# First expert of a mixture layer by block products, last feed-forward group reordered by token block, token sums spread over the expert's units

## The chip, the cores and the metric

One core of a Trainium2 chip (trn2). The metric is the device time of one execution in microseconds (us). An execution of the kernel before takes 1540.04 us, the median of three (1538.99 to 1540.66).

## The reference, cut to what matters

The kernel computes three layers in a row on 1536 tokens of width 512. The attention ahead of them is not touched by the change.

```python
def _moe_ref(x, w_in, w_out):            # 512 -> 2048 -> 512
    h = x @ w_in
    sp = np.where(h > 20.0, h, np.log1p(np.exp(np.minimum(h, 20.0))))
    return (h * np.tanh(sp)) @ w_out     # "Mish"

def _moe2_ref(x, w_gate, w1, w2):        # N=1536, D=512, E=8 experts, F=1024
    logits = x @ w_gate
    logits = logits - logits.max()
    P = np.exp(logits)
    for _ in range(8):
        P /= P.sum(1, keepdims=True) + 1e-09
        P /= P.sum(0, keepdims=True) + 1e-09
        P *= N / E
    out = np.zeros((N, D))
    for e in range(E):
        out += P[:, e:e + 1] * (np.maximum(x @ w1[e], 0.0) @ w2[e])
    return out
```

The loop of eight rounds divides the 1536 x 8 table P by its row sums and then by its column sums. It is called the normalisation below.

## The kernel before, in words

Numbers are fp32, split into a high and a low fp32r part; a product of two numbers is three matmuls (high x high, high x low, low x high). The program is written out by hand, with one in-order queue for each engine: PE (matmuls), DVE, ACT, POOL, and SP for DMAs.

**Attention** ends at about 267 us and leaves the tokens in `xh` and `xl` (4 chunks of 128 features x 1536 tokens).

**Steps.** The feed-forward layer (16 chunks of 128 hidden features) and the first of the eight experts (8 chunks) run as steps. A step is one chunk i and one block tb of 512 tokens: `up(n)` issues 12 matmuls of 128x512, `act(n)` forms the hidden values (ACT) and their low part `gl` (DVE), and three steps later (LAG) `down(n)` issues 12 matmuls into four PSUM banks y0 to y3. Four chunks make a group, and the steps run over groups, then token blocks, then chunks: 48 steps of the layer and 24 of the first expert. After the last chunk of a group `evacuate` adds the four banks to `acc` (DVE). After the last group of the layer, `split` writes the new `xh` (ACT) and `xl` (POOL).

The layer's weights are 64-bit numbers that are decoded on the way (`decode`: 2 ACT, 5 DVE and 1 POOL operation for half a chunk), and put as two parts into one of eight ring buffers (`convert_hi` on ACT, `convert_lo` on POOL). The table `early` says in which step that is done.

`at(n, f)` appends work to the end of step n. In the steps of the first expert stand: the eight matmuls of `logits` for each token block, the eight rounds of the normalisation on 32 partitions (`sinkhorn`, one round in each step), `spread` (four DMAs that bring P to 128 partitions), and `make_t`, which forms the sums and differences of tokens ("T" factors) that the next part needs.

**Units.** The other seven experts run by block products: of each group g of 768 tokens and each quarter k of an expert's hidden features, `product` computes seven products (six matmuls of 128x384 each) in place of eight, into two PSUM banks; after each, `post` reads its bank (ACT: `p1`, `c11`; DVE: `u`, `v`, `c22`, `c21`, `c12`). A bank is used by every second product, so product 3 waits until `u` was read after product 1, product 5 until `v` was read after product 3, and so on. DVE then forms four low parts (`rest`, tile `gl`), and `second` issues 36 matmuls of 128x512 into six banks. An expert's four units end with six `gather` (P times bank, added to `acc`). There are 56 units: seven experts for 768 tokens, then the same for the other 768. The weights of a unit are prepared one or two units ahead (`unit_a`, `unit_s`, `unit_w`: copies on ACT, sums and low parts on POOL). `job(u, s, f)` appends work behind product s of unit u (s from 0 to 6), or behind quarter s - 7 of its `second`.

Units and steps use the same PSUM banks and, for the even units, ring buffers 0 to 2.

Of the kernel before, what the change touches and what calls it, by code (L numbers as in the profile page):

```python
# [61 lines left out]
def lsh_attention_moe_kernel(  # L62
# [780 lines left out]
    def act(n):  # L843
        g = step(n)[0]
# [3 lines left out]
        if g < NG:  # L848
            a = t_p.tile([P, TB], F32, tag="t", name="t")
            nc.scalar.activation(a, t, AF.Mish)  # L850
            nc.scalar.copy(hi, a)  # L851
            nc.vector.tensor_sub(lo, a, f32(hi))  # L852
        else:
            nc.scalar.activation(hi, t, AF.Relu)
            nc.vector.scalar_tensor_tensor(
                out=lo, in0=t, scalar=0.0, in1=f32(hi), op0=ALU.max, op1=ALU.subtract
            )
        hid[n] = (hi, lo)

    def down(n):  # L860
# [3 lines left out]
        for j in range(KC):  # L864
# [4 lines left out]
            if g < NG:  # L869
                ops = [(w0[:, c], hi), (w0[:, c], lo), (w1[:, c], hi)]  # L870
            else:
                ops = [(hi[:, c], w0), (hi[:, c], w1), (lo[:, c], w0)]
            for m, (x, y) in enumerate(ops):
# [487 lines left out]
```

## Time and profile before

| what | us |
|---|---|
| median of three executions | 1540.04 |
| the profiled execution: its time | 1540.54 |
| the profiled execution: span of its instructions | 1538.7 |
| PE busy in the span | 1524.6 (99%) |
| DVE, ACT, POOL busy | 879.9, 677.8, 880.3 |
| chain that ended last, by engine | PE 92%, DVE 3%, DMA 2% |

Busy times are sums over the span. The chain is followed back from the last instruction: at each step to what released it. In rows of the trace the columns are the start in us from the span's first instruction, the duration in us, the engine and line, the operation, out<-in, the shape, and in brackets how long the engine was idle ahead of it and who ended that.

### The profile page before, as it was taken

Reading aid. Unit: us, or ns where it says so; the run is one execution under the profiler, and the core shown is the slowest. Engines: PE = TensorE matmul, PEld = TensorE weight load, DVE = VectorE, ACT = ScalarE, POOL = GpSimd, SP = SyncE. Lnnn points to the kernel's source line nnn. Section 1 sums busy time; section 2 is a strip of 40 time slices with the busy share of each in tenths; the row PEclk is TensorE's granted clock in tenths of the full one; section 3 lists DMA queues with packets and bytes.
Section 4 is the critical chain, followed back from the end, with each engine's and each line's share of the span. In section 5 each row is a group of like instructions: output and inputs, shape, how many; then the busy total and the mean of one; then the engine's idle time right before and its main releaser. Section 6 shows DMA issues by size and latency. Waiting matters only on the chain.

```text
span 1538.7 us, 20305 instructions
## 1 busy us (share of the span) xinstructions
PE 1524.6 (99%) x7444; PEld 1341.9 (87%) x7444; DVE 879.9 (57%) x1434; ACT 677.8 (44%) x1230; POOL 880.3 (57%) x729
## 2 busy tenths in 40 slices
PE   9999999999999999999999999999999999999999
PEld 7798888888888788889999998989898989898998
DVE  8899995846663238666444454676534444445353
ACT  5777777654433232233434333333433333333331
POOL 6798977333324230266666666666666666666661
PEclk9999999999999999999999999999999999999999
DMA  7755550122221000112222222222322222221211
GB/s 184 160 138 148 140 133 16 55 71 67 69 69 55 28 28 1 29 56 69 69 69 69 69 69 69 69 69 69 110 69 69 68 66 67 65 67 68 69 56 41
DMA packets 64387, 113.50 MB, mean 74 GB/s; under 512 B 19792, under 2 KB 20792, under 8 KB 64288
## 3 DMA queue, kind: packets, MB, share of 16 engines
q1 hardware_dynamic: 62688, 112.17, 25.2%
q8 instruction: 58, 0.95, 0.3%
q14 instruction: 41, 0.34, 0.1%
q10 hardware_dynamic: 1600, 0.05, 0.0%
HBM read 89.22 MB, written 3.15 MB: 60 GB/s over the span
## 4 chain that ended last, share of the span: by engine, by line
PE 92%; DVE 3%; DMA 2%; POOL 1%; issue 1%; ACT 1%; SPq 0%; DVEq 0%; ACTq 0%; POOLq 0%
PE y L1224 30%; PE u L1157 27%; PE y L874 13%; PE pav L496 5%; PE h L840 4%; PE h L838 4%; PE h L839 4%; PE pst L446 1%; PE pst L447 1%; PE ps L394 1%; DMA vt<-in_v_dram 1%; DVE mx L408 1%; DMA raw<-in_qk_dram 1%; POOL plo L458 0%; PE lg L900 0%
## 5 line engine op out<-in xcount | busy, mean ns | idle before, releaser
L1165 ACT ACTIVATE gh<-c 128x384 fp32r<-128x384 f32 x224 | 117.8, 526 | 153.1 <-DVE c L1177 151.3
L1177 DVE TENSOR_TENSOR u<-u,p 128x384 f32<-128x384 f32 x56 | 31.2, 558 | 264.3 <-PE u L1157 264.3
L1170 DVE SCALAR_TENSOR_TENSOR gl<-c,gh 128x384 fp32r<-128x384 f32 x224 | 170.0, 820 | 0.0
L1224 PE MATMUL y<-ww,gh 128*128 128x512 f32 x672 | 163.4, 391 | 0.0
L1224 PE MATMUL y<-w,gh 128*128 128x512 f32 x672 | 162.6, 391 | 0.0
L458 POOL TENSOR_TENSOR plo<-p,ph 128x384 fp32r<-128x384 f32 x128 | 138.8, 1096 | 33.0 <-ACT ph L455 19.1
L1224 PEld LDWEIGHTS y<-w,gh 128*128 128x128 f32 x672 | 125.8, 188 | 25.1
L1224 PEld LDWEIGHTS y<-ww,gh 128*128 128x128 f32 x672 | 125.8, 188 | 25.1
L153 POOL TENSOR_TENSOR stage<-stage,sgn 128x512 f32<-128x512 f32 x32 | 43.1, 1346 | 120.8 <-DVE sgn L151 113.4
L1046 POOL TENSOR_TENSOR w<-stage,w 128x1024 fp32r<-128x1024 f32 x28 | 67.0, 2392 | 78.4 <-ACT w L1042 78.4
L874 PE MATMUL y<-gh,w 128*128 128x512 f32 x336 | 110.3, 389 | 0.0
L452 ACT ACTIVATE p<-pst 128x384 f32<-128x384 f32 x192 | 92.6, 487 | 38.3 <-PE pst L447 32.3
L1046 POOL TENSOR_TENSOR ww<-stage,ww 128x1024 fp32r<-128x1024 f32 x28 | 67.2, 2402 | 72.6 <-ACT ww L1042 72.6
L1039 POOL TENSOR_TENSOR w<-sraw,w 128x1024 fp32r<-128x1024 f32 x28 | 68.6, 2448 | 67.7 <-ACT w L1035 67.7
L408 DVE TENSOR_REDUCE mx<-ps 128x1 f32<-128x768 f32 x95 | 90.1, 948 | 15.5 <-PE ps L394 14.8
L838 PE MATMUL h<-xh,w 128*128 128x512 f32 x252 | 98.4, 391 | 0.0
L840 PE MATMUL h<-xh,w 128*128 128x512 f32 x252 | 98.2, 390 | 0.1
L839 PE MATMUL h<-xl,w 128*128 128x512 f32 x252 | 98.1, 389 | 0.0
L1022 POOL TENSOR_TENSOR wa<-stage,wa 128x512 fp32r<-128x512 f32 x28 | 40.2, 1436 | 96.8 <-ACT wa L1017 69.1
L852 DVE TENSOR_TENSOR gl<-t,gh 128x512 fp32r<-128x512 f32 x48 | 47.7, 994 | 77.5 <-ACT gh L851 77.5
L1042 ACT CAST ww<-stage 128x1024 fp32r<-128x1024 f32 x28 | 29.4, 1051 | 141.0 <-PE y L1224 141.0
L1042 ACT CAST w<-stage 128x1024 fp32r<-128x1024 f32 x28 | 29.4, 1050 | 138.2 <-PE y L1224 138.2
(243 smaller groups left out, 4069.1 us busy)
## 6 DMA issues: line engine op xcount, KB each, us to landing
stage<-in_w_dram SPq DMA_DIRECT2D x152, 512.0 KB
raw<-in_qk_dram SPq DMA_DIRECT2D x13, 384.0 KB
wx<-hi SPq DMA_DIRECT2D x20, 192.0 KB
vt<-in_v_dram SPq DMA_DIRECT2D x16, 192.0 KB
out_dram<-acc SPq DMA_DIRECT2D x11, 256.0 KB
zq<-hi SPq DMA_DIRECT2D x11, 192.0 KB
ak<-hi SPq DMA_DIRECT2D x11, 192.0 KB
zq<-lo SPq DMA_DIRECT2D x11, 192.0 KB
```

The source lines that it names most:

```text
L408: nc.vector.tensor_reduce(out=m[:, t, 0:1], in_=s_t[t][:, :, :HALF], axis=AX.XY, op=ALU.max, negate=True)
L452: nc.scalar.activation(p_t[u, c], st_t.pop((u, c))[:, :HALF], AF.Exp, scale=0.125)
L458: (nc.gpsimd if e == "P" else nc.vector).tensor_sub(out, in0, in1)
L838: nc.tensor.matmul(t, wt[:, 0, f], xh[:, kc, c], start=(kc == 0), stop=False)
L839: nc.tensor.matmul(t, wt[:, 0, f], xl[:, kc, c], start=False, stop=False)
L840: nc.tensor.matmul(t, wt[:, 1, f], xh[:, kc, c], start=False, stop=(kc == KC - 1))
L874: nc.tensor.matmul(yps[j], x, y, start=(head and m == 0), stop=(tail and m == 2))
L1046: nc.gpsimd.tensor_sub(y[:, 1, :], t, f32(y)[:, 0, :])
L1157: nc.tensor.matmul(bank[x], weight(u, a, m, kc), moving(u, b, mm, kc), start=(first and n == 0), stop=(n == 5), skip_group_check=not first)
L1165: nc.scalar.activation(hi, src, AF.Relu)
L1170: nc.vector.scalar_tensor_tensor(out=lo, in0=src, scalar=0.0, in1=f32(hid_u[u, c][0]), op0=ALU.max, op1=ALU.subtract)
L1224: nc.tensor.matmul(y_t[t], (hi, hi, lo)[m][:, t % 3 * P:(t % 3 + 1) * P], y, start=(k == 0 and first), stop=(k == NF // 2 - 1 and last),)
```

## The change

The first expert leaves the steps and joins the units: 48 steps remain, and 64 units (first expert first). The last two groups of the layer run over token blocks 0 and 1 first, and then both over block 2. The T factors of the first 768 tokens, which come from blocks 0 and 1, are made during steps 43 to 48. The logits of block 2, and the normalisation, now on 128 partitions and split into a half for rows (4 DVE operations) and a half for columns (13 DVE operations, eight of them transpositions of 32x32), stand in units 0 to 6. P is final in unit 6, so for the first 768 tokens the first expert's banks are stored as they are and scaled by six `scale_first` in unit 7; for the others `gather` multiplies at once. `spread` is gone. The decode table steps by 1.35 steps for half a chunk instead of 1.5.

```diff
-    NW = N64 + NF
-    NU = 2 * (E - 1) * NF // 2
+    NU = 2 * E * NF // 2
...
-    GROUPS = [list(range(i, i + FG)) for i in range(0, NW, FG)]
-    steps = [(g, tb, i) for g, c in enumerate(GROUPS) for tb in range(NTB) for i in c]
+    GROUPS = [list(range(i, i + FG)) for i in range(0, N64, FG)]
+    turns = [(g, tb) for g in range(NG - 2) for tb in range(NTB)]
+    turns += [(g, tb) for g in (NG - 2, NG - 1) for tb in range(2)] + [(g, 2) for g in (NG - 2, NG - 1)]
+    steps = [(g, tb, i) for g, tb in turns for i in GROUPS[g]]
...
     def across(x, op, negate=False):
-        y, r = small("y", Q), small("r")
-        nc.vector.transpose(out=y, in_=x)
+        y, r = small("y", Q, P), small("r", Q)
+        for a, part in enumerate(quarters(x)):
+            nc.vector.transpose(out=y[:, a * Q:(a + 1) * Q], in_=part)
         nc.vector.tensor_reduce(out=r, in_=y, axis=AX.X, op=op, negate=negate)
         return r
...
     def sinkhorn_max():
+        m = small("m", P)
+        nc.vector.tensor_reduce(out=m, in_=prob, axis=AX.XY, op=ALU.max)
+        r = across(m.to_broadcast([P, Q]), ALU.max, negate=True)
+        m = small("nm", P)
+        for part in quarters(m):
+            nc.vector.tensor_copy(part, r)
+        return m
...
-    for it in range(8):
-        at(n0 + 3 + it, sinkhorn)
-    at(n0 + 12, spread)
+    done_at = {tb: n + LAG for n, (g, tb, _) in enumerate(steps) if g == NG - 1}
+    for tb in range(NTB - 1):
+        at(done_at[tb] + 3, logits, tb)
...
-    for x in range(8):
-        at(t0 + 4 + x, make_t, (1, 2, 4, 3)[x % 4], x // 4)
+    for n, k, kc in ((1, 1, 0), (2, 2, 0), (2, 4, 0), (3, 3, 0), (4, 1, 1), (4, 2, 1), (5, 4, 1), (6, 3, 1)):
+        at(done_at[1] + n, make_t, k, kc)
+    at(free[RING] - 2, unit_s, 0)
+    for f, i in ((unit_w_hi, 0), (unit_w_lo, 0), (unit_s_hi, 1), (unit_s_lo, 1), (unit_a_hi, 2), (unit_a_lo, 2)):
+        at(free[RING + i] + 1, f, 0)
+    at(free[RING + 2] + 2, unit_s, 1)
...
-                nd += 1.5
+                nd += 1.35
...
+        if e == 0:
+            nc.vector.tensor_scalar(out=dst, in0=y_t[t], scalar1=prob[:, i, 0:1] if g else 1.0, scalar2=None, op0=ALU.mult)
+            return
...
-    for i in range(NT):
-        job(i // 3, NP1 + 1 + i % 3, scale_first, i)
+    job(0, NP1 + 1, logits, NTB - 1, ps_u, "u0")
+    job(0, NP1 + 2, put("m", sinkhorn_max))
+    job(1, 0, lambda: sinkhorn_exp(box["m"]))
+    for x in range(16):
+        job(1 + x // 3, (2, NP1 + 1, NP1 + 1)[x % 3], (sinkhorn_rows, sinkhorn_cols)[x % 2])
+    for i in range(NT // 2):
+        job(7, NP1 + i // 3, scale_first, i)
```

So the row and column halves alternate: units 1 to 5 hold three halves each, one behind product 2 and two behind the second quarter of `second`, and unit 6 the last one. Behind product 2 stands a row half in units 1, 3 and 5, and a column half in units 2, 4 and 6.

**First place: DVE, the end of the steps.** Of the changed program, from the T factors of steps 47 and 48 (`t`, `tw`) over the last evacuation (`acc`) to the first operation of unit 0 (`u`). Lines are those of the changed file.

```order
L983 TENSOR_TENSOR t<-xh,xl 128x384
L984 TENSOR_TENSOR t<-t 128x384
L989 TENSOR_TENSOR tw<-t,tw 128x384
L978 TENSOR_TENSOR t<-xh 128x384
L979 TENSOR_TENSOR t<-xl 128x384
L980 TENSOR_TENSOR t<-t 128x384
L989 TENSOR_TENSOR tw<-t,tw 128x384
L866 TENSOR_TENSOR acc<-y_5699,acc 128x512
L866 TENSOR_TENSOR acc<-y_5703,acc 128x512
L866 TENSOR_TENSOR acc<-y_5707,acc 128x512
L866 TENSOR_TENSOR acc<-y_5711,acc 128x512
L1152 TENSOR_TENSOR u<-u,p_5813 128x384
```

The order of the kinds is that of before, where the T factors were spread over eight steps, of which the last was the last step with an `up`; now they are packed into six steps, of which the last has only a `down`.

**Second place: ACT, the same stretch.** From the last two steps with an `up` (L841 is Mish, L842 the high part `gh`) over the copies of T factors (L988) and of unit 0's weights (L996, L997) and the new `xh` of block 2 (L871) to `p1`, the copy after product 0 (L1159).

```order
L841 ACTIVATE t<-h 128x512
L842 CAST gh<-t 128x512
L988 CAST tw<-t 128x384 x2
L996 CAST wx_78<-stage 128x512
L997 CAST wx_78<-stage 128x256
L841 ACTIVATE t<-h 128x512
L842 CAST gh<-t 128x512
L988 CAST tw<-t 128x384 x2
L871 CAST xh<-acc 128x512 x4
L1159 COPY p_5813<-u 128x384
```

Before, the same place reads so:

```order
L854 ACTIVATE gh<-h 128x512
L1009 CAST tw<-t 128x384
L1184 COPY p_6728<-u 128x384
```

Four copies that each read one addition of the last evacuation now stand ahead of `p1`.

**Third place: DVE in units 0 to 2.** First from the end of unit 0 (the logits `lg`, their maximum, `nm` as the offset of the exponential) to `u` of unit 1, and then from `u` to `v` of unit 2.

```order
L887 STREAM_TRANSPOSE lgs<-lg 32x128 x4
L888 TENSOR_TENSOR prob<-lgs 128x32
L905 TENSOR_REDUCE m<-prob 128x1
L899 STREAM_TRANSPOSE y<-m 32x32 x4
L900 TENSOR_REDUCE r<-y 32x1
L909 COPY nm<-r 32x1 x4
L1152 TENSOR_TENSOR u<-u,p_5987 128x384
```

```order
L1152 TENSOR_TENSOR u<-u,p_6141 128x384
L923 TENSOR_REDUCE csum<-prob 128x8
L899 STREAM_TRANSPOSE y<-csum 32x32 x4
L900 TENSOR_REDUCE r<-y 32x1
L925 TENSOR_SCALAR r<-r 32x1
L926 RECIPROCAL r<-r 32x1
L929 STREAM_TRANSPOSE i<-r 32x32 x4
L930 SCALAR_TENSOR_TENSOR prob<-i,prob 128x96
L1152 TENSOR_TENSOR v<-u,p_6141 128x384
```

Before, `v` followed `u` at once in every unit (but for one `gather` where an expert had just ended).

## Rows read from the trace of the kernel before

**Rows 1.** The page, part 1: busy us, share of the span, instructions.

```profile
PE 1524.6 (99%) x7444; PEld 1341.9 (87%) x7444; DVE 879.9 (57%) x1434; ACT 677.8 (44%) x1230; POOL 880.3 (57%) x729
```

**Rows 2.** Waits of PE: us in total, times, longest; first of ten rows.

```profile
PE prow L427 <- DVE col L415: 2.5, 4, 1.3
```

**Rows 3.** Busy time by stretch: the steps, then the units.

```profile
267.10:665.10 398.00, 397.91 (x1754) 327.09 (x1753) 223.33 (x374) 152.03 (x242) 114.74 (x70) 1.00 0.15 46
665.10:1538.70 873.60, 869.75 (x4370) 788.27 (x4368) 429.09 (x631) 330.14 (x564) 552.39 (x436) 1.00 0.22 69
```

**Rows 4.** Timeline, PE: product 0 and product 5 of the first unit, product 0 of the last.

```profile
665.17 0.33 PE L1157 MATMUL u<-xh,wx 128*128 128x384 f32 x1
...
670.40 1.20 PE L1157 MATMUL u<-tw,wx 128*128 128x384 f32 x6
...
1519.18 0.33 PE L1157 MATMUL u<-xh,wa 128*128 128x384 f32 x1
```

**Rows 5.** Timeline, DVE and ACT: last evacuation, then `p1`, `u`, `v` of the first unit.

```profile
663.33 2.73 DVE L884 TENSOR_TENSOR acc<-y,acc 128x512 f32<-128x512 f32 x4 [4.79 <-PE y L874]
...
666.43 0.48 ACT L1184 COPY p<-u 128x384 f32<-128x384 f32 x1 [8.49 <-PE u L1157]
...
667.54 0.56 DVE L1177 TENSOR_TENSOR u<-u,p 128x384 f32<-128x384 f32 x1 [1.48 <-PE u L1157]
...
669.56 0.56 DVE L1177 TENSOR_TENSOR v<-u,p 128x384 f32<-128x384 f32 x1 [1.46 <-PE u L1157]
```

**Rows 6.** Groups by line and form, ACT, 500 to 700 us: busy us, mean ns | idle.

```profile
L890 ACT CAST xh<-acc 128x512 fp32r<-128x512 f32 x8 | 5.0, 622 | 1.3 <-DVE acc L887 1.0
L1009 ACT CAST tw<-t 128x384 fp32r<-128x384 f32 x8 | 4.1, 513 | 24.9 <-DVE t L1005 13.0 <-DVE t L1001 11.9
L850 ACT ACTIVATE t<-h 128x512 f32<-128x512 f32 x4 | 2.4, 598 | 15.8 <-PE h L840 15.8
L1017 ACT CAST wa<-stage 128x512 fp32r<-128x512 f32 x2 | 1.2, 614 | 0.0
```

**Rows 7.** Timeline, DVE and POOL: a `make_t` that meets `unit_s`.

```profile
634.76 1.76 DVE L999 TENSOR_TENSOR t<-xh 128x384 f32<-128x384 f32 x1
...
639.12 1.13 DVE L1010 TENSOR_TENSOR tw<-t,tw 128x384 fp32r<-128x384 f32 x1 [0.58 <-ACT tw L1009]
...
637.18 0.94 POOL L1030 TENSOR_TENSOR sraw<-sraw,stage 128x256 f32<-128x256 f32 x1
```

**Rows 8.** One line each, DVE: duration ns min/median/max, first and last start.

```profile
L950 DVE TENSOR_SCALAR acc<-acc,prob x12: 474/960/2612, 677.2 to 727.6; 128x512 f32<-128x512 f32 x12
L455 DVE CAST ph<-p x29: 311/492/1273, 34.7 to 264.9; 128x384 fp32r<-128x384 f32 x29
L522 DVE STREAM_TRANSPOSE rs<-nr x16: 557/566/579, 59.6 to 270.4; 128x384 f32<-128x384 f32 x16
```

**Rows 9.** POOL: busy in a stretch; one row; groups by line, 500 to 720 us.

```profile
670.60:695.20 24.60, 24.36 (x17) 1.00 0.33 104
...
681.77 2.59 POOL L1039 TENSOR_TENSOR w<-sraw,w 128x1024 fp32r<-128x1024 f32 x1
...
L891 POOL TENSOR_TENSOR xl<-acc,xh 128x512 fp32r<-128x512 f32 x8 | 10.6, 1353 | 23.5 <-ACT xh L890 23.5
```

**Rows 10.** Groups by line and form, DVE, 500 to 700 us: the normalisation.

```profile
L934 DVE TENSOR_REDUCE csum<-pr 32x8 f32<-32x384 f32 x8 | 7.0, 875 | 0.3
L930 DVE TENSOR_REDUCE rsum<-pr 32x48 f32<-32x384 f32 x8 | 4.2, 530 | 0.0
L940 DVE SCALAR_TENSOR_TENSOR pr<-i,pr 32x384 f32<-32x384 f32 x8 | 4.4, 547 | 0.3
L915 DVE STREAM_TRANSPOSE y<-csum 32x32 f32<-32x32 f32 x8 | 1.6, 200 | 0.3
L916 DVE TENSOR_REDUCE r<-y 32x1 f32<-32x32 f32 x9 | 1.6, 174 | 0.3
L937 DVE RECIPROCAL r<-r 32x1 f32<-32x1 f32 x8 | 1.2, 151 | 0.3
```

More of the change, by code (lines that the diff above doesn't have):

```diff
@@ L162, in source @@
     def source(i):
-        return dec[i % NDEC] if i < N64 else staged[i]
+        return dec[i % NDEC]
     def convert_hi():
@@ L847, in act @@
         lo = g_p.tile([P, TB], F32R, tag="gl", name="gl")
[L848 to L857, printed above, removed]
+        a = t_p.tile([P, TB], F32, tag="t", name="t")
+        nc.scalar.activation(a, t, AF.Mish)
+        nc.scalar.copy(hi, a)
+        nc.vector.tensor_sub(lo, a, f32(hi))
         hid[n] = (hi, lo)
@@ L868, in down @@
             w0, w1 = wt[:, 0, 512:1024], wt[:, 1, 512:1024]
[L869 to L873, printed above, removed]
+            for m, (x, y) in enumerate(((w0[:, c], hi), (w0[:, c], lo), (w1[:, c], hi))):
                 nc.tensor.matmul(yps[j], x, y, start=(head and m == 0), stop=(tail and m == 2))
@@ L937, in sinkhorn @@
         nc.vector.reciprocal(out=c, in_=c)
[L938 to L939 removed]
+        i = small("i", P, Q)
+        for part in quarters(i):
+            nc.vector.transpose(out=part, in_=c.to_broadcast([Q, Q]))
         nc.vector.scalar_tensor_tensor(
[L941 removed]
+            out=prob, in0=i[:, 0:E].unsqueeze(1).to_broadcast([P, NT, E]), scalar=float(NTOK // E), in1=prob, op0=ALU.mult, op1=ALU.mult
         )
[L944 to L946 removed]
     def scale_first(i):
@@ L965, in lsh_attention_moe_kernel @@
     LAG = 3
-    blk = NTB * NF
-    start_e = NG * NTB * FG
-    for tb in range(NTB):
-        n0 = start_e - (NTB - 1 - tb) * FG + LAG + 2
-        at(n0, logits, tb)
-    at(n0 + 1, put("m", sinkhorn_max))
-    at(n0 + 2, lambda: sinkhorn_exp(box["m"]))
-    for it in range(8):
-        at(n0 + 3 + it, sinkhorn)
-    at(n0 + 12, spread)
+    done_at = {tb: n + LAG for n, (g, tb, _) in enumerate(steps) if g == NG - 1}
+    for tb in range(NTB - 1):
+        at(done_at[tb] + 3, logits, tb)
     tw = []
@@ L1081, in lsh_attention_moe_kernel @@
     convert_lo()
-    for i in range(RING_A + NX + 1, NW):
+    for i in range(RING_A + NX + 1, N64):
         need = free[i - RING] + 1 if i >= RING else 0
-        if NATT <= i < N64:
+        if NATT <= i:
             nd = max(nd, free_dec.get(i - NDEC, 0))
@@ L1105, in lsh_attention_moe_kernel @@
                 decode(*t)
-        first = n >= LAG and step(n - LAG)[0] < NG and step(n - LAG)[4]
+        first = n >= LAG and step(n - LAG)[4]
         if first:
@@ L1120, in lsh_attention_moe_kernel @@
             f()
-    assert not side, side.keys()
+    assert not side and not early and not later, (side.keys(), early.keys())
     blocks.close()
@@ L1132, in lsh_attention_moe_kernel @@
     ))
+    sk_p.append(pool("sk", bufs=1))
+    wide_t = lambda: sk_p[0].tile([P, TB], F32, tag="wide", name="lgs")
     def weight(u, name, m, kc):
```

81 lines of the change are left out of this document (27 added, 54 removed).

## The prediction

> **What bounds the kernel now.** I read the busy times first: PE works 99% of the span [rows 1]. Then PE's waits: the largest of ten entries is 2.5 us, all of them in the attention [rows 2]. Then the two stretches that the change touches: in the steps PE is busy 397.9 of 398.0 us, and in the units nothing but the end is idle [rows 3]. So PE is the bound, it never waits there, and any wait that the change makes adds to the time in full. Work on the other engines is free only while it keeps inside the gaps that PE leaves it, so the question is how wide these gaps are.
>
> In a unit they are narrow. Product 5 starts 5.23 us after product 0 [rows 4], so a product takes 1.05 us, and product 3 starts at 3.14. `u` ends at 2.93 and `v` at 4.95, counted from the unit's start [rows 5]. Product 5 overwrites what `v` reads, so `v` has 0.28 us to spare. Work that is put between `u` and `v` on DVE is free up to 5.23 - 0.1 for the hand-over - 0.56 - 2.93 = 1.64 us. Beyond that, each us costs one.
>
> **What is gained.** The steps issue 72 x 24 matmuls, and 24 of the logits, in 398.0 us [rows 3]: 0.2272 us each. The first expert's 24 steps are 576 matmuls, 130.9 us. Eight units replace them at (1519.18 - 665.17) / 55 = 15.53 us each [rows 4], 124.2 us. The gain is 6.6 us. The logits cost the same wherever they stand.
>
> **The end of the steps.** Call T the end of the last `down`. Before, the last evacuation starts 1.84 us ahead of it and ends 0.89 behind it [rows 5]; `p1` runs at once when product 0 is done. Product 2 needs `p1`, at T + 2.1.
> Now the queue ahead is fuller (first and second place). Step 46 evacuates too; it ends 8.2 + 5.45 = 13.6 us ahead of T (three steps with only `down`, one full step), and by the same pattern DVE is free from T - 12.7. From there it has two `gl` at 0.69 (as an addition of the same size [rows 5]) and 14 operations of T factors at 0.56 (as `u` [rows 5]): 9.2 us. To it come waits:
> - four times 0.58 us for the ACT copy in a `make_t` [rows 7]: 2.3;
> - step 47's `gl`: on ACT its Mish and copy stand behind the last T copy and the two copies of `unit_a` (0.61, some 0.4, 0.60, 0.62 [rows 6]); DVE has only 0.56 us to do meanwhile, so it waits 1.7;
> - POOL: where a `make_t` met `unit_s`, its four operations took from 634.76 to 640.25, 5.5 us instead of 2.8 [rows 7]. The four operations of `unit_s` of unit 1 meet the last seven here. In those rows the tail of a longer POOL operation is in the first 1.76 us; without it I take 1.7, between 0 and 2.7.
>
> So the last evacuation starts at -12.7 + 9.2 + 2.3 + 1.7 + 1.7 = T + 2.2 and ends at T + 4.9. Now the copy of `xh` (0.62 [rows 6]) and `p1` (0.48 [rows 5]) follow: T + 6.0 instead of T + 2.1. **PE waits 3.9 us**; 2.2 without POOL, 4.9 with all of it.
>
> **From unit 0 to unit 1.** With that wait and 1.8 us of logits, unit 0 lasts 21.2 us, and unit 1's product 3 wants `u` read at T + 24.4. The logits end at T + 3.9 + 7.3 + 4.1 + 1.8 = T + 17.1. Four transpositions (about 0.3 each, between 32 and 384 columns [rows 8, 10]), the maximum, four more and a reduction bring DVE, with 0.03 between operations, to T + 20.0; the addition and the four copies to `nm` alone would end by T + 20.6. That is in time.
> But POOL does not pause there. Before, it was busy 24.4 of 24.6 us from 670.6 on, T + 5.4 to T + 30 [rows 9], and the change puts four more subtractions of 1.35 us in front [rows 9]. DVE operations that copy or scale from SBUF to SBUF, or read two SBUF tiles, wait for a running POOL operation: scaling takes 0.47 us alone and 2.61 beside a POOL operation of 2.59 us [rows 8, 9], and a cast from 0.31 to 1.27 [rows 8]. Transpositions don't: 16 of them, in a stretch where POOL is mostly busy, took 557 to 579 ns [rows 8]. The addition and the four copies are five operations of the waiting kinds, and each meets one POOL operation, of 24.36 / 17 = 1.43 us on average [rows 9]: 7.2 us, `u` ends at T + 28.4, and **PE waits 4.1 us**. No row shows a copy of one element beside POOL; if such a copy is too small to wait, the cost is 0. I take 4.1, since the nearest row, the cast, waits.
> [...]
>
> **Column halves between `u` and `v`** (third place; units 2, 4, 6). The price of a column half: the reduction of 96 elements 0.32 (0.875 for 384 [rows 10], with the 0.15 of the smallest operation as the fixed part), eight transpositions at 0.20 + 0.03, a reduction 0.17, two of 0.15, the product of 96 elements 0.25 (0.547 for 384, same fixed part), and gaps: 3.0 us. Two of the 13 are of the waiting kinds; `unit_s` runs there in pieces of about 0.74, so I add 0.2. The room is 1.64: **1.55 us in each of three units, 4.65 us**. In unit 4 a `gather`, about 0.7 us, stands ahead of it: **0.7 more**. Ends: 0.5 us each, if transpositions overlap, and 3.2 each, if both of them wait for a whole piece of 0.9.
>
> **The rest.** A row half (four operations, 0.95 us) fits into 1.64; with its two waits for POOL it is slightly late: 0.1 in units 1, 3 and 5, 0.3 in all; at most 0.8 each. Two halves behind the second quarter of `second` are 4.0 us and start some 11 us into the unit, with 6.9 us until the next `u`: 0, and if POOL's longest operation (2.6 us) is met, still 0. Six `scale_first` in unit 7: 6 x 0.47 and waits of 3.6 us are 6.4, in the same room: 0. The 12 new stores by `gather` stand where other experts' stand: 0. The decode's faster pace has its last chunk converted in step 33 and used in step 35: a full step of 5.4 us as cover, else that much is lost. Eight more 512 KB loads at the units' usual rate, with DMA at 22% [rows 3]: 0.
>
> **Sum:** -6.6 + 3.9 + 4.1 + 4.65 + 0.7 + 0.3 = +7.0 us. Against the profiled execution, 1540.54, that is 1547.5; it lies 0.5 over the median, so against the median **1547.0 us**.
>
> **The rivals.**
> *Small operations are cheap.* The copies to `nm` don't wait, and transpositions run into each other. Then 0 and 0.5 x 3 + 0.7 stay of the second and third cost, and the sum is -6.6 + 3.9 + 2.2 + 0.3 = -0.2: 1539.8. For it: transpositions are independent, and the four additions of the last evacuation took 2.73 us, a little less than four of 0.69. Against it: the cast's row. Chance 0.17.
> *The halves are covered, faster.* One thing decides: whether a further transposition costs about 0.06 us instead of 0.23. Then a column half is 1.6 us and fits into the 1.64, unit 4 keeps 0.7, and the copies, small as well, cost 0. If POOL is not met at the end of the steps either: -6.6 + 2.2 + 0.7 = -3.7, 1536.3. For it: units carry gathers today without a wait of PE. Against it: 0.20 us for a block of 32 columns is nearly all fixed cost [rows 10]. Chance 0.10.
> [...]
> *Weights or decode come late.* Unit 0's weights are made only in steps 44 to 46, when their ring buffers fall free, and the decode has one step of cover. If either is missed: 5.4 us more, 1552.4. For it: the DVE and ACT queues of the first place are those that it needs. Against: `a_lo`, the last part, should end some 5 us ahead of T. Chance 0.06.
>
> **The numbers.** The forecast has 0.67. A measurement of this kernel can tell some 0.2%, 3.1 us, from no change. The forecast's own range is 1543.5 to 1550.5, by the ends above (a column half between 0.5 and 2.4, the boundary between 2.2 and 4.9, `u` of unit 1 between 2 and 5). To hold 8 in 10 the range takes in the first rival and ends at 1538.5 and 1551.0. Faster by 0.2%: most of the second rival, 0.08. Within 0.2%: the first rival and the forecast's edge, 0.18. Slower: 0.74.
>
> **What would show it.** In the profile of the changed kernel PE should wait behind the attention for the first time: product 2 of unit 0 for ACT's `p1` (3.9 us), product 3 of unit 1 for DVE's `u` (4.1), product 5 of units 2, 4 and 6 for `v` (1.5 to 2.3), and none in units 8 to 63. Copies to `nm` that take 0.1 us beside a busy POOL, or column halves of 2 us, would prove me wrong on the second and third term; a last evacuation that starts ahead of T on the first.

## The result and the profile after

The changed kernel takes 1549.11 us, the median of six executions (1546.75 to 1550.68), beside 1539.73 us for the kernel before on the same chip: a ratio of 1.0060, 95% interval 1.0047 to 1.0073. It is slower, by 9.4 us.

First the top of the page of the changed kernel and the first rows of its waits (what waits, for whom: us in total, times, longest). They answer to [rows 1] and [rows 2].

```profile
span 1546.9 us, 20639 instructions
PE 1523.6 (98%) x7492; PEld 1349.4 (87%) x7492; DVE 915.4 (59%) x1540; ACT 695.0 (45%) x1266; POOL 941.0 (61%) x785
```

```profile
PE u L1132 <- DVE v L1152: 4.5, 4, 1.8
PE u L1132 <- ACT p L1159: 3.7, 1, 3.7
...
PE u L1132 <- DVE u L1152: 2.1, 2, 1.0
```

PE's busy time is about what it was, yet the span is 8.2 us longer: three entries of waits have appeared behind the attention. They add up to 10.3 us.

To place them, I take the start of each unit's product 0 from PE's rows; the difference to the next one is how long the unit lasted. Without a wait a unit lasts 15.53 us [rows 4], and unit 0, with eight matmuls of 0.2272 for the logits of block 2, 17.35. The last column is the stretch from the first matmul of the steps to the last instruction, since the attention's end lies between 264.7 and 269.6 us in the profiled executions, though its code is the same in all.

| kernel | unit 0 | 1 | 2 | 3 | 4 | 5 | 6 | from the steps on |
|---|---|---|---|---|---|---|---|---|
| before | | | | | | | | 1271.6 |
| changed | 24.10 | 16.27 | 16.95 | 16.83 | 17.64 | 16.83 | 16.95 | 1280.3 |
| no wait at all | 17.35 | 15.53 | 15.53 | 15.53 | 15.53 | 15.53 | 15.53 | |

From unit 7 on every unit lasts 15.51 to 15.54 us. So the loss lies in the first seven: 125.57 - 110.53 = 15.0 us, against a gain that was foreseen as 6.6 us and came out as 6.4.

**Unit 0** lost 6.75 us. PE's rows around product 2 (start, duration, line, operation, shape; in brackets the idle time ahead of it and who ended that):

```profile
533.24 1.20 PE L1132 MATMUL u<-tw,w 128*128 128x384 f32 x6
538.19 0.69 PE L1132 MATMUL u<-xh,wx 128*128 128x384 f32 x1 [3.74 <-ACT p L1159]
...
540.28 4.01 PE L1132 MATMUL u<-tw,w 128*128 128x384 f32 x12
```

PE's clock in stretches (busy us and count of each engine, then the granted clock, the DMA share and rate):

```profile
532.00:538.00 6.00, 2.45 (x14) 2.09 (x12) 4.49 (x9) 3.17 (x6) 1.96 (x2) 0.94 0.00 0
538.00:546.00 8.00, 7.81 (x29) 7.81 (x30) 2.23 (x4) 3.48 (x8) 7.92 (x7) 0.62 0.20 60
546.00:556.00 10.00, 10.00 (x46) 7.63 (x45) 9.07 (x19) 3.72 (x6) 9.92 (x8) 1.00 0.24 70
```

The wait for `p1` is there, 3.74 us. Then something follows that I had not reckoned with: the granted clock falls to 0.62 over 8 us. In stretches of 0.5 and 1 us it reads 0.50 from 538.0 to 544.0, 0.89 in the next and 1.00 from 544.5 on. Six matmuls took 1.20 us ahead of the wait, twelve take 4.01 behind it. That is the other 3.0 us of unit 0. In this execution the fall cost more than in others: in runs 3, 4, 6, 8 and 10 below, whose unit 0 has the same wait (3.74 to 3.87 us), it lasts 22.96 to 23.11 us, which leaves 1.9 us for the clock. Why `p1` was late stands in the rows of DVE and ACT:

```profile
534.63 2.48 DVE L866 TENSOR_TENSOR acc<-y,acc 128x512 f32<-128x512 f32 x4
```

```profile
535.35 2.41 ACT L871 CAST xh<-acc 128x512 fp32r<-128x512 f32 x4 [1.23 <-DVE acc L866]
537.66 0.47 ACT L1159 COPY p<-u 128x384 f32<-128x384 f32 x1
```

The evacuation starts 2.5 us behind the last `down` (before, 1.84 us ahead of its end [rows 5]), and on ACT the copies to `xh` hold `p1` back.

**Units 2, 4 and 6** lost 1.4, 2.1 and 1.4 us, units 3 and 5 lost 1.3 each. Of unit 2, DVE between `u` and `v`, and the row on which unit 3's `u` waits:

```profile
575.39 0.32 DVE L923 TENSOR_REDUCE csum<-prob 128x8 f32<-128x96 f32 x1
575.75 0.85 DVE L899 STREAM_TRANSPOSE y<-csum 32x32 f32<-32x32 f32 x4
...
577.30 0.85 DVE L929 STREAM_TRANSPOSE i<-r 32x32 f32<-32x32 f32 x4
...
578.48 0.55 DVE L1152 TENSOR_TENSOR v<-u,p 128x384 f32<-128x384 f32 x1
...
585.94 2.14 DVE L920 TENSOR_TENSOR prob<-prob,rsum 128x96 f32<-128x96 f32 x1
...
590.91 2.40 DVE L930 SCALAR_TENSOR_TENSOR prob<-i,prob 128x96 f32<-128x96 f32 x1
593.24 0.54 DVE L1152 TENSOR_TENSOR u<-u,p 128x384 f32<-128x384 f32 x1
```

```profile
585.58 2.39 POOL L1018 TENSOR_TENSOR w<-sraw,w 128x1024 fp32r<-128x1024 f32 x1
590.82 2.38 POOL L1025 TENSOR_TENSOR w<-stage,w 128x1024 fp32r<-128x1024 f32 x1 [2.86 <-ACT w L1021]
```

A column half fills 575.39 to 578.48, 3.1 us, and `v` follows it. Behind the second quarter a row and a column half each have one product with two SBUF operands; alone they take 0.26 us, as the first does at 571.92 with POOL idle, and here 2.14 and 2.40, until POOL's operation ends. So `u` of unit 3 ends at 593.78 instead of some 592.4.

**Unit 1** lost 0.74, at `v`. The copies to `nm`, for which I had 4.1 us, do not wait:

```profile
555.54 0.62 DVE L909 COPY nm<-r 32x1 f32<-32x1 f32 x4
```

```profile
553.95 2.39 POOL L1018 TENSOR_TENSOR w<-sraw,w 128x1024 fp32r<-128x1024 f32 x1
```

Four copies in 0.62 us, all of them while POOL was busy (until 556.34).

### The profile page after: what moved, and what is told of

It reads as the page before. It is cut to its first block, busy times and chain, and to the rows that moved or that the text cites. A ratio compares the mean times of both kernels' runs of the same rounds, so it can differ in the third digit from the quotient of the medians.

```text
span 1546.9 us, 20639 instructions
## 1 busy us (share of the span) xinstructions
PE 1523.6 (98%) x7492; PEld 1349.4 (87%) x7492; DVE 915.4 (59%) x1540; ACT 695.0 (45%) x1266; POOL 941.0 (61%) x785
## 4 chain that ended last, share of the span: by engine, by line
PE 89%; DVE 7%; issue 1%; ACT 1%; POOL 1%; DMA 0%; DVEq 0%; ACTq 0%; POOLq 0%
PE y L1199 33%; PE u L1132 29%; PE y L856 8%; PE pav L488 5%; PE h L833 3%; PE h L831 3%; PE h L832 3%; PE ps L386 2%; PE pst L438 2%; PE pst L439 1%; DVE mx L400 1%; DMA vt<-in_v_dram 0%; DVE gl L1145 0%; POOL plo L450 0%; PE lg L881 0%
## 5 line engine op out<-in xcount | busy, mean ns | idle before, releaser
L1145 DVE SCALAR_TENSOR_TENSOR gl<-c,gh 128x384 fp32r<-128x384 f32 x256 | 194.4, 821 | 0.0
L1199 PE MATMUL y<-ww,gh 128*128 128x512 f32 x768 | 186.6, 391 | 0.0
L1199 PE MATMUL y<-w,gh 128*128 128x512 f32 x768 | 185.8, 391 | 0.0
L1199 PEld LDWEIGHTS y<-w,gh 128*128 128x128 f32 x768 | 143.7, 188 | 28.9
L1199 PEld LDWEIGHTS y<-ww,gh 128*128 128x128 f32 x768 | 143.7, 188 | 28.8
L1001 POOL TENSOR_TENSOR wx<-stage,wx 128x512 fp32r<-128x512 f32 x32 | 45.2, 1413 | 91.0 <-ACT wx L996 91.0
L1199 PE MATMUL y<-ww,gl 128*128 128x512 f32 x384 | 98.2, 389 | 0.0
L1199 PE MATMUL y<-w,gl 128*128 128x512 f32 x384 | 97.4, 389 | 0.0
L1132 PE MATMUL u<-tw,ws 128*128 128x384 f32 x480 | 91.8, 336 | 2.1 <-DVE u L1152 2.1
L1132 PE MATMUL u<-tw,w 128*128 128x384 f32 x480 | 93.5, 341 | 0.0
```

The costliest lines, as they stand in the source:

```text
L1001: nc.gpsimd.tensor_sub(a[:, 1, 0:512], t[:, 0, :], f32(a)[:, 0, 0:512])
L1132: nc.tensor.matmul(bank[x], weight(u, a, m, kc), moving(u, b, mm, kc), start=(first and n == 0), stop=(n == 5), skip_group_check=not first)
L1145: nc.vector.scalar_tensor_tensor(out=lo, in0=src, scalar=0.0, in1=f32(hid_u[u, c][0]), op0=ALU.max, op1=ALU.subtract)
L1199: nc.tensor.matmul(y_t[t], (hi, hi, lo)[m][:, t % 3 * P:(t % 3 + 1) * P], y, start=(k == 0 and first), stop=(k == NF // 2 - 1 and last),)
```

## The experiments

All start from the changed kernel. The kernel before took 1540.2 us (median) beside runs 1 to 4, 1541.0 beside 5 to 8 and 1539.6 beside 9 and 10, so runs are compared by their ratio to it, by the unit lengths and by the last column of the table behind the tenth. The unit lengths are those of one profiled execution of each run.

**1. The sums of unit 1's weights moved out of the last steps.**

```diff
-    at(free[RING + 2] + 2, unit_s, 1)
...
-        job(0, 0 if f in (unit_a_hi, unit_a_lo) else 3, f, 1)
+        job(0, 0 if f in (unit_a_hi, unit_a_lo) else 5, f, 1)
+    job(0, -1, unit_s, 1)
...
-            job(u, 0 if u else 4, unit_s, u + 2)
+            job(u, 0 if u else 5, unit_s, u + 2)
```

> The four POOL sums of unit 1's weights leave the last steps and stand behind POOL's token parts in unit 0 (the weight copies that need them move by two products). Theory: beside POOL four DVE operations of the last T factors took 1.09 to 1.14 us instead of 0.56 and 0.69; without it the last evacuation starts 2.0 us earlier, PE waits 1.7 instead of 3.7 us ahead of product 2 of unit 0, and after so short a wait the granted clock stays at 1.00, which saves 3.0 more: 5.0 us less than the changed kernel, 1544.1. Rival 1: the clock falls to the same share whatever the wait: 2.0 less, 1547.1. Rival 2: the DVE operations wait for something else than POOL: no change, 1549.1.

Measured: 1547.33 us (1545.08 to 1549.63), ratio 1.0044, 1.0032 to 1.0056. Its waits, and the clock in the same stretches as above:

```profile
PE u L1131 <- DVE v L1151: 5.6, 4, 1.8
...
PE u L1131 <- ACT p L1158: 2.2, 1, 2.2
```

```profile
532.00:538.00 6.00, 3.79 (x16) 3.47 (x15) 3.22 (x6) 3.62 (x7) 4.40 (x4) 0.81 0.00 0
538.00:546.00 8.00, 8.00 (x40) 7.41 (x39) 4.87 (x7) 5.17 (x9) 7.41 (x8) 0.93 0.17 46
```

The wait fell by 1.5 us, not 2.0, so POOL is part of the lateness; the rest of the 2.0 stayed, since the `gl` ahead of the T factors still meets POOL's part of unit 0's weights and takes 1.13 us as before. The clock fell behind 2.2 us of waiting too: my theory's second half is wrong, the number is the first rival's, and unit 0 gained only 2.7. Of that, unit 1 gave 1.1 back: its wait for `v` grew. That is the first sign that the wait in unit 0 had covered something in unit 1. By the times alone this run is not apart from the changed kernel (1.0044 and 1.0060, with overlapping intervals); the gain is read from the traces.

**2. The wait filled with matmuls.**

```diff
...
         for s in range(NP1):
+            if u == 0 and s == 2:
+                y_t[0] = ps_z.tile([P, 512], F32, tag="z0", name="y")
+                for x in range(16):
+                    nc.tensor.matmul(y_t[0], xh[:, 0, 0:P], xh[:, 0, 0:512], start=True, stop=True)
             product(u, s)
```

> Sixteen matmuls of 128x512 whose result is overwritten are put ahead of product 2 of unit 0, where PE waits 3.7 us; the wait itself stays. Theory: the granted clock of 0.62 in 538.2 to 546.0 comes from the idle stretch ahead of it. With PE at work there it stays at 1.00 and unit 0 lasts 21.1 instead of 24.1 us: 3.0 less, 1546.1. Rival: the clock falls for another reason: no change, 1549.1.

Measured: 1545.77 us (1545.48 to 1547.01), ratio 1.0038, 1.0026 to 1.0050. The added matmuls, the same twelve matmuls as above, and the clock:

```profile
533.45 3.83 PE L1280 MATMUL y<-xh 128*128 128x512 f32 x16
...
538.51 2.24 PE L1132 MATMUL u<-tw,w 128*128 128x384 f32 x12
```

```profile
538.00:546.00 8.00, 8.00 (x43) 7.30 (x42) 4.80 (x7) 5.44 (x10) 7.84 (x7) 1.00 0.24 67
```

The theory holds. PE does useless work as long as it waited before, and the kernel is 3.3 us faster: the twelve matmuls take 2.24 instead of 4.01 us, and unit 0 lasts 21.5 instead of 24.1. The fall of the clock was the price of idling, on top of the idling itself.

**3. No rounds.** The two lines that place the 16 halves are taken out.

> Leaves out the eight rounds of the normalisation (all 16 halves); the exponential stays. Theory: all that units 1 to 6 last beyond 15.53 us is the halves' work and waits: they take 15.5 each, 8.3 us less in sum, 1540.8; unit 0 stays at 24.1. Rival: the 1.3 us each in units 3 and 5 comes from weights or gathers and stays: 5.7 less, 1543.4.

Measured: 1539.28 us (1537.42 to 1541.16), ratio 0.9996, 0.9987 to 1.0005. Units 1 to 6 last 15.51 to 15.54: all that they lost, 8.3 us, came from the halves and their waits. Unit 0 lasted 22.98, where 24.1 was expected; the clock fell there too, for a shorter time. The rival is out: weights and gathers are in time.

**4. POOL's long operations in two.**

```diff
-        nc.gpsimd.tensor_sub(s[:, 1, :], sraw, f32(s)[:, 0, :])
+        for c in (slice(0, 512), slice(512, 1024)):
+            nc.gpsimd.tensor_sub(s[:, 1, c], sraw[:, c], f32(s)[:, 0, c])
...
-        nc.gpsimd.tensor_sub(y[:, 1, :], t, f32(y)[:, 0, :])
+        for c in (slice(0, 512), slice(512, 1024)):
+            nc.gpsimd.tensor_sub(y[:, 1, c], t[:, c], f32(y)[:, 0, c])
```

> POOL's low parts of the sums and of the second weights (one operation of 128x1024, 2.4 us) are made by two operations of half the width, in all units. Theory: u of units 3 and 5 was late because the row and the column half ahead of it each waited for the end of one long POOL operation (2.14 and 2.40 us); with half the length these waits halve and units 3 and 5 last 15.5 to 15.7 instead of 16.8: 2.2 to 2.6 us less, 1546.7; the other units as they were. Rival: DVE waits until POOL pauses, not until one operation ends: the waits stay, 0, 1549.1.

Measured: 1545.98 us (1544.07 to 1549.62), ratio 1.0039, 1.0026 to 1.0051. The rows of unit 2 that answer to those of the changed kernel:

```profile
584.23 1.03 DVE L920 TENSOR_TENSOR prob<-prob,rsum 128x96 f32<-128x96 f32 x1
...
588.09 0.26 DVE L930 SCALAR_TENSOR_TENSOR prob<-i,prob 128x96 f32<-128x96 f32 x1
590.15 0.56 DVE L1154 TENSOR_TENSOR u<-u,p 128x384 f32<-128x384 f32 x1 [1.80 <-PE u L1134]
```

```profile
583.86 2.55 POOL L1019 TENSOR_TENSOR w<-sraw,w 128x512 fp32r<-128x512 f32 x2
```

The waits fall from 2.14 and 2.40 to 1.03 and nothing, DVE is idle for 1.80 us ahead of `u`, and units 3 and 5 last 15.60. The first product ends at 585.26, when the first of POOL's two pieces is done and the second, until 586.41, is running: DVE waits for the running operation, not for a pause. The second product now comes early enough to run while POOL is idle (586.41 to 589.10). Unit 1 gains 0.67 for the same reason; units 2, 4 and 6 keep their loss, as expected, since it is work and not waiting. Of the 4.3 us by which the last column falls, 1.0 is unit 0's shorter fall of the clock, which runs 3, 8 and 10 show without this edit.

**5. The boundary cleared.** The four banks' pool stays open, and their last evacuation and the copies stand inside unit 0.

```diff
+    ps_y = ctx.enter_context(tc.tile_pool(name="ps_y", bufs=1, space=bass.MemoryType.PSUM))
     ps_h = blocks.enter_context(tc.tile_pool(name="ps_h", bufs=3, space=bass.MemoryType.PSUM))
     ps_x = blocks.enter_context(tc.tile_pool(name="ps_x", bufs=1, space=bass.MemoryType.PSUM))
-    ps_y = blocks.enter_context(tc.tile_pool(name="ps_y", bufs=1, space=bass.MemoryType.PSUM))
...
-        if tail:
+        if tail and n < NST - 1:
             for j in range(KC):
                 evacuate(g, tb, j)
...
+    for j in range(KC):
+        job(0, 1 if j < 2 else 4, evacuate, NG - 1, NTB - 1, j)
+    for j in range(KC):
+        job(0, 2 if j < 2 else 5, split, j)
     for f in (unit_a_hi, unit_a_lo, unit_s_hi, unit_s_lo):
-        job(0, 0 if f in (unit_a_hi, unit_a_lo) else 3, f, 1)
+        job(0, 0 if f in (unit_a_hi, unit_a_lo) else 6, f, 1)
...
-            job(u, 0 if u else 4, unit_s, u + 2)
+            job(u, 0 if u else 6, unit_s, u + 2)
```

> The last evacuation and the copies that split its tokens are taken out of the queue between the last T factors and unit 0: two of the four evacuations stand behind u and two behind c22 of unit 0, the copies behind c11 and c21; the weight copies of unit 1 follow three products later; the four banks are those of the same pool as before. Theory: p1 and u were late only because these operations stood ahead of them on ACT and DVE. p1 is then ready 0.3 us late instead of 3.7, PE never waits 2 us there, so the granted clock stays at 1.00, and unit 0 lasts 17.4 to 18 instead of 24.1 us: 6 to 6.7 less, 1542.7; the end of unit 0 comes nearer to the logits' chain, which may give 1 back in unit 1, as the first run did. Rival: the T factors themselves are late (tw of the last one), the wait moves to product 3 and keeps 2 us and the clock loss with it: 3 less at most, 1546.

Measured: 1551.46 us (1548.87 to 1553.43), ratio 1.0067, 1.0055 to 1.0080: no faster. Unit 0 lasts 17.77, as the theory says; 6.3 us are gained there. But unit 1 lasts 21.63 instead of 16.27. ACT, DVE and PE in unit 1:

```profile
555.68 1.28 ACT L913 ACT_TABLE_LOAD   x1
556.98 0.38 ACT L913 ACTIVATE prob<-prob,nm 128x96 f32<-128x96 f32 x1
```

```profile
557.38 0.25 DVE L917 TENSOR_REDUCE rsum<-prob 128x12 f32<-128x96 f32 x1 [1.13 <-ACT prob L913]
557.67 2.26 DVE L918 TENSOR_SCALAR rsum<-rsum 128x12 f32<-128x12 f32 x1
...
560.23 2.09 DVE L920 TENSOR_TENSOR prob<-prob,rsum 128x96 f32<-128x96 f32 x1
562.24 0.55 DVE L1152 TENSOR_TENSOR v<-u,p 128x384 f32<-128x384 f32 x1
```

```profile
562.84 1.37 PE L1132 MATMUL u<-tw,wa 128*128 128x384 f32 x4 [3.68 <-DVE v L1152]
```

The first row half stands between `u` and `v` and needs the exponential, which stands behind a table load of 1.28 us, and then meets two long POOL operations: 2.26 and 2.09 us where the changed kernel had 0.68 and 0.60. PE waits 3.68 us and its clock falls again (0.67 from 562.8 to 568.0). What the long unit 0 had covered is POOL's queue. From the start of unit 0 to the end of its second long operation (`w<-stage,w`) POOL needs 27.8 us in the changed kernel, 27.7 in the first run and 26.8 here, so a unit 0 that is 6.3 us shorter puts the row half of unit 1 beside POOL's long operations instead of behind them. The edit also moves copies and POOL operations into unit 0 and makes `p1` of unit 1 0.3 us late; how much of the 5.4 us is due to that was not separated. Another 2.3 us went at the start of the steps, by the new order of the pools, and 1.0 in the steps; the seventh run's rows show it.

**6. Halves in smaller pieces,** with the edit of the fourth run.

```diff
...
-    for x in range(16):
-        job(1 + x // 3, (2, NP1 + 1, NP1 + 1)[x % 3], (sinkhorn_rows, sinkhorn_cols)[x % 2])
+    for x in range(24):
+        u, s = divmod(x + 1, 4)
+        job(1 + u, NP1 + 1 if s else 2, (sinkhorn_rows, put("c", cols_sum), put("d", cols_mul, "c"))[x % 3])
```

> POOL's pieces as in the fourth run, and each column half is cut in two (sums, first four transpositions, reciprocal; then four transpositions and the product). Of the 24 pieces three stand behind the second quarter of units 1 to 6 and one behind product 2 of units 2 to 7, so that no whole column half stands between u and v. Theory: beyond the fourth run's gain, units 2, 4 and 6, which lasted 17.1, 17.8 and 17.1 us there, fall to 15.5, and where the first part of a column half (1.9 us by its rows) stands between u and v 0.3 us remain (units 3 and 6), 0.3 in unit 4 for its gather: 4.3 less than the fourth run, 1541.7. Rival: three pieces behind the quarter and their waits for POOL end too late for the next u: units 3 to 7 lose 1 us each, 1546.

Measured: 1541.50 us (1540.39 to 1543.22), ratio 1.0004, 0.9995 to 1.0013, 5.4 us less than the fourth run by the ratios and 3.5 by the last column. Of the waits behind the attention one longer than 0.2 us is left:

```profile
PE u L1134 <- ACT p L1161: 3.9, 1, 3.9
```

Units 1 to 6 last 15.54, 15.59, 15.65, 16.41, 15.59 and 15.65: only unit 4, with its gather, keeps 0.9. Three pieces behind one quarter are not too many.

**7. The fifth and sixth together.**

> The fifth and the sixth run's edits together. Theory: the gains lie in different units and add: 1549.1 - 6.4 - 7.0 = 1535.7, below the kernel before (1539.7 to 1540.2). Rival: part of one was cover for the other (a later u in unit 1 because unit 0 is shorter): 1537 to 1539.

Measured: 1538.73 us (1537.16 to 1543.64), ratio 0.9992, 0.9982 to 1.0002: 3 us above the expectation, and inside the rival's 1537 to 1539. Unit 1 does lose something (units 0 and 1 last 17.91 and 16.66), at `p1` and a `gl` and not at `u`, but most of the 3 us is a wait that is new:

```profile
PE h L831 <- DVE rs L496: 2.3, 1, 2.3
```

The first step waits for the end of the attention, as in the fifth run. The pool of the four banks is opened first here, which moves the banks of `up`, and the wait for an operation of the attention (`rs`) is new. The clock falls behind it as well:

```profile
267.30:272.00 4.70, 4.70 (x14) 3.74 (x15) 2.61 (x7) 1.94 (x3) 0.96 (x2) 0.64 0.02 3
```

That is 1.0 us more (the steps last 266.6 instead of 265.6). The fifth run has the same wait and the same 266.6.

**8. Waits made on purpose,** by reductions ahead of `u` in four later units.

```diff
...
         elif s == 1:
+            for x in range({16: 3, 22: 5, 36: 7, 44: 9}.get(u, 0)):
+                nc.vector.tensor_reduce(out=rs, in_=f32(xh)[:, 0, 0:512], axis=AX.X, op=ALU.add)
             total("u", b, val["p1"])
```

> Adds 3, 5, 7 and 9 reductions of 128x512 ahead of u in units 16, 22, 36 and 44, where PE has no wait and every clock reading is 1.00; PE should then wait about 1.6, 2.8, 4.0 and 5.2 us at product 3. Theory: the fall of the clock follows from an idle stretch of 2 us or more, wherever it stands: the first unit lasts only its wait longer, the other three 1 to 3 us more than their wait. Rival: it belongs to the change from steps to units, and each unit lasts just its wait longer.

One execution, 1562.38 us. Units 16, 22, 36 and 44 lasted 16.19, 15.54, 20.62 and 21.85 us. PE's first row behind the wait in unit 36, and the clock in three stretches (unit 4, unit 16, and unit 36 behind the wait):

```profile
1116.71 3.69 PE L1133 MATMUL u<-tw,w 128*128 128x384 f32 x12 [3.26 <-DVE u L1153]
```

```profile
612.00:618.00 6.00, 4.16 (x18) 3.74 (x17) 4.75 (x14) 1.05 (x2) 1.84 (x3) 0.80 0.31 90
...
802.00:810.00 8.00, 7.62 (x40) 6.98 (x40) 6.75 (x12) 4.35 (x8) 4.48 (x6) 1.00 0.21 66
...
1117.00:1121.00 4.00, 4.00 (x16) 4.00 (x16) 1.44 (x4) 0.00 (x0) 0.00 (x0) 0.57 0.02 9
```

The waits came out smaller than I sized them: DVE did the reductions early, while it was idle (unit 22 had none of it). Unit 36 waited 3.26 us and lasted 5.1 longer; unit 44 waited 4.70 and lasted 6.3 longer. The clock's share is thus 1.8 and 1.6 us, far from the steps: the fall follows from the idling, and not from the place. Unit 4, whose wait of 1.84 us is the changed kernel's own, lost the clock here (0.80, and the unit lasted 19.20), while in the changed kernel's profile it kept it after 1.80 us (17.64). In the fourth run the same unit kept it even after 1.98 us (the clock is 1.00 from 610.7 to 616.0, and the unit lasted 17.79):

```profile
610.75 1.32 PE L1134 MATMUL u<-tw,wx 128*128 128x384 f32 x6 [1.98 <-DVE v L1154]
```

Behind about 2 us of idling both happen, and the longer wait is not always the one that costs.

**9. The waits removed.** The seventh run, with the pool of the four banks kept in its old place, and:

```diff
-            job(u, NP1 + 1, unit_s_hi, u + 2)
+            job(u or 1, NP1 + 1 if u else 0, unit_s_hi, u + 2)
...
-            job(u, NP1 + 1, unit_s_lo, u + 2)
+            job(u or 1, NP1 + 1 if u else 0, unit_s_lo, u + 2)
-    job(1, 0, lambda: sinkhorn_exp(box["m"]))
+    job(1, 2, lambda: sinkhorn_exp(box["m"]))
...
-            settle(s in (0, 2, 4, 5))
+            settle((s in (0, 2, 4, 5)) + (u == 4) * ((s == 5) - (s == 2)))
```

> The seventh run with three mends, each for a wait that its trace shows: the four banks keep their old places (there the steps started 2.3 us late, since their first banks were those that the attention reads last); in unit 1 the copy of unit 2's sums stands behind p1 and the exponential behind product 2, so that p1 is not 0.3 us late; in unit 4 the gather behind product 2 moves behind product 5. Theory: the three give 2.3, up to 0.9 and 0.75 back, and what remains beyond 15.53 us in units 0 to 6 is some 1.4: 1538.7 - 3.9 = 1534.8, 5 to 6 below the kernel before. Rival: in unit 1 the exponential now delays another copy on ACT and unit 1 stays at 16.7: 1535.7; or the attention's 2.3 us came from something else than the banks: 1537.1.

Measured: 1534.48 us (1533.24 to 1535.15) beside 1539.56, ratio 0.9965, 0.9952 to 0.9979. It beats both kernels. The first step's wait is gone (so it was the banks), and so is the one in unit 4 (15.90 instead of 16.40). Unit 1 still lasts 16.65, as the rival had it, though for another reason; the edit there gave nothing. `p1` is in time now, but PE waits for a `gl`: the four `gl` of unit 1 take 5.71 us beside POOL's operations (3.06 in unit 2). Behind the attention these waits are left:

```profile
PE y L1201 <- DVE gl L1147: 0.5, 1, 0.5
...
PE u L1134 <- ACT p L1161: 0.2, 1, 0.2
```

```profile
556.22 5.71 DVE L1147 SCALAR_TENSOR_TENSOR gl<-c,gh 128x384 fp32r<-128x384 f32 x4
```

**10. Copies of three sizes.**

```diff
             nc.vector.tensor_copy(part, r)
+        y, z = prob[0:Q].rearrange("p t e -> p (t e)"), small("z", P, Q)
+        for n in (1, 2, Q):
+            for part in quarters(z):
+                nc.vector.tensor_copy(part[:, 0:n], y[:, 0:n])
```

> The changed kernel with twelve copies more behind those to nm, each of 32 partitions: four of 1 element, four of 2, four of 32 (their results are not used). Theory: a copy of one element does not wait for a running POOL operation and the others do: 0.15 us each for the first four, while the first of 2 elements, and most of the following, last until POOL's operation of 0.7 to 2.4 us ends; u of unit 1 is then late by 2 us or more. Rival: 32 partitions make the difference, and all twelve take 0.14 to 0.17 us beside a busy POOL: some 1.9 us more on DVE, unit 1 at most 1 us longer.

One execution, 1554.81 us. The copies by shape (count, then busy us and mean ns), one of two elements in time, and POOL around it:

```profile
L913 DVE COPY z<-prob 32x2 f32<-32x2 f32 x4 | 2.8, 702 | 0.1
L913 DVE COPY z<-prob 32x32 f32<-32x32 f32 x4 | 2.1, 517 | 0.1
L913 DVE COPY z<-prob 32x1 f32<-32x1 f32 x4 | 0.6, 144 | 0.1
```

```profile
559.60 2.30 DVE L913 COPY z<-prob 32x2 f32<-32x2 f32 x1
```

```profile
556.75 2.41 POOL L1022 TENSOR_TENSOR w<-sraw,w 128x1024 fp32r<-128x1024 f32 x1
559.50 2.37 POOL L1029 TENSOR_TENSOR w<-stage,w 128x1024 fp32r<-128x1024 f32 x1 [0.34 <-ACT w L1025]
```

The four added copies of one element took 144 ns each, as did the four to `nm`; all eight ran between 557.66 and 558.96, beside POOL's operation of 2.41 us. Of the four of two elements two fell into POOL's pause and took 0.16; the first took 0.19, until just behind the end of POOL's operation (559.16); the last met the next operation and took 2.30, until it ended. Of those of 32 elements three take 0.59 to 0.66, each until one of POOL's pieces of 0.7 ends, and one, between two pieces, takes 0.17. It is the size, not the 32 partitions: one element did not wait in eight of eight copies, and two did, though the case for two rests mainly on the one copy of 2.30 us. `u` of unit 1 came late by this, and the unit lasted 20.60 us.

The unit lengths of the profiled executions:

| run | unit 0 | 1 | 2 | 3 | 4 | 5 | 6 | from the steps on |
|---|---|---|---|---|---|---|---|---|
| 1 sums later | 21.41 | 17.36 | 16.98 | 16.81 | 17.61 | 16.83 | 16.93 | 1278.7 |
| 2 wait filled | 21.46 | 16.61 | 16.93 | 16.83 | 17.63 | 16.83 | 16.96 | 1277.9 |
| 3 no rounds | 22.98 | 15.51 | 15.51 | 15.51 | 15.54 | 15.51 | 15.51 | 1270.3 |
| 4 POOL pieces | 23.09 | 15.60 | 17.11 | 15.60 | 17.79 | 15.60 | 17.11 | 1276.0 |
| 5 boundary | 17.77 | 21.63 | 16.95 | 16.81 | 17.63 | 16.81 | 16.96 | 1280.5 |
| 6 halves in pieces | 23.11 | 15.54 | 15.59 | 15.65 | 16.41 | 15.59 | 15.65 | 1272.5 |
| 7 all three | 17.91 | 16.66 | 15.79 | 15.65 | 16.40 | 15.59 | 15.65 | 1269.1 |
| 8 made waits | 22.96 | 16.27 | 16.96 | 16.81 | 19.20 | 15.51 | 16.96 | 1291.7 |
| 9 waits removed | 17.91 | 16.65 | 15.83 | 15.63 | 15.90 | 15.59 | 15.68 | 1267.8 |
| 10 copy sizes | 22.99 | 20.60 | 16.93 | 16.83 | 17.63 | 16.83 | 16.93 | 1283.2 |

## Why the prediction was right, and where its sum was not

The time was foreseen as 1547.0 and is 1549.11, inside the range and on the side that had 0.74. The sum of +7.0 stands against +8.7 in the traces (1280.3 - 1271.6). Its terms fared differently:

- **The gain, -6.6: right, -6.4.** 48 steps and 16 matmuls of logits take 265.6 us instead of 398.0, and a unit lasts 15.53 us where nothing waits (units 1 to 7 in the third run); with the last eight matmuls of logits that is 265.6 + 124.2 + 1.8 - 398.0.
- **The end of the steps, 3.9: right, 3.74.** The last evacuation starts at T + 2.5 (foreseen T + 2.2). The parts hold too: four waits of 0.58 us for the ACT copy, 1.42 us ahead of step 47's `gl` (foreseen 1.7), and 2.0 us by which four DVE operations are longer beside POOL (foreseen 1.7), of which the first run took 1.5 away. Taking evacuation and copies out of the way left 0.3 us of the wait (fifth run).
- **What the wait does to the clock, nothing in the sum: 3.0 us missed** (1.9 in five other profiles with the same wait). I wrote that any wait adds to the time in full, and took that for the whole price. The second and eighth run show that PE can be slower after an idle stretch as well (twelve matmuls in 4.01 us behind the wait, in 2.24 where it was filled). No row of before had a wait of this length in front of dense matmuls behind the attention [rows 2].
- **`u` of unit 1, 4.1: wrong, 0.** The step that failed is "I take 4.1, since the nearest row, the cast, waits". The bound of 0 that I gave with it was the truth, and the sign that I had named for being wrong on this term came: about 0.1 us a copy beside a busy POOL. The tenth run shows where the border lies: a copy of two elements lasted up to 2.30 us. The copies of one element, 141 to 148 ns beside a busy POOL in the two profiles, did not wait.
- **Column halves between `u` and `v`, 4.65 + 0.7: right.** Units 2, 4 and 6 last 1.42, 2.11 and 1.42 longer, against 1.55, 2.25 and 1.55; that is 4.95 against 5.35 in sum. A transposition costs 0.21 us from one to the next (0.85 for four), with no overlap. So the second rival fell, and of the first the half on transpositions, while its half on copies was right.
- **Two halves behind the second quarter, 0: wrong, 1.3 in units 3 and 5.** The step that failed is "if POOL's longest operation (2.6 us) is met, still 0". It is met twice, once by each half: 2.14 + 2.40 us. I had 2.9 us of room and one wait of 2.6. The fourth run, with shorter operations on POOL, takes the loss away.
- **Row half in unit 1, 0.1: 0.74,** inside its end of 0.8. The two waits for POOL were in the term; the exponential, with a table load of 1.28 us ahead of it, had not been put on that path, and DVE waits 0.53 us for it. In units 3 and 5, for which I had 0.1 each, `v` is in time. With the short unit 0 of the fifth run PE waits 3.7 us at this place.

So 4.1 us that did not come were made good by 3.0 of clock, 2.6 in units 3 and 5 and 0.6 in unit 1. As measured the terms add up: -6.36 + 3.74 + 3.01 + 4.95 + 2.60 + 0.74 = +8.7. That the size came out near is luck: two terms that the sum did not have stood in for one that did not come. The terms that were right alone give -6.4 + 3.7 + 4.95 = +2.3, slower, but within the 3.1 us that I had called too small to tell; so the mechanism carried the sign and not the clear slowdown. The range has a slip that changed nothing: the upper end of a column half is 3.2 in its own term and 2.4 in the range. Neither weights nor decode came late, so the third rival fell: the steps last 265.6 us, and in the third run every unit behind unit 0 lasts 15.51 to 15.55 us.

What is left in the ninth run can be read from its trace: the 0.6 us of unit 0 is mostly `p1`, which stands on ACT behind the copy for the last T factor, and the 1.1 us of unit 1 is the `gl` beside POOL. What stays open: what decides whether the clock falls behind a wait near 2 us was not tried, and how the loss of unit 1 in the fifth run divides between the shorter unit 0 and the work that was moved.

## What to carry to other kernels

Where one engine is busy all the time, price a wait of it at the wait and its aftermath (3.74 us and up to 3.0 more here), and look for what stands behind the wait: here the queue of another engine was hardly shorter when the wait was gone, and PE waited 3.7 us in the next unit. Count how often each small operation can meet a long one of another engine whose end it then waits for (twice behind one quarter here, 2.14 and 2.40 us), not whether it can; cutting the long operation in two was the cheap remedy here (1.03 us and nothing). An idea that loses may only be badly placed: the same change, with the halves and POOL's operations cut, the boundary cleared and the banks kept, is 0.35% (0.21 to 0.48) faster than the kernel before, which had no waits there for these edits to remove [rows 3].
